# Bank-to-bank copies in 15 groups, an 18th group, one start per bank, and a new order of work

## The chip, the core and the metric

The kernel runs on one core of a Trainium2 chip. The engines of the core are PE (TensorE, the matrix products), DVE (VectorE), ACT (ScalarE), POOL (GpSimd, here the queue that issues the loads) and SP (SyncE, here the queue of the transposes by DMA and of the stores). PE writes its sums into PSUM, which has 8 banks; DVE and ACT read them there and can write there too. The metric is the device time of one execution in microseconds.

## The reference

Attention of 4 batches with 8 heads over 768 tokens, in which a token sees the first 8 tokens and the last 96, with a bias by distance, and then a feed-forward layer with a squared relu:

```python
scores = scale * np.matmul(q, k.transpose(0, 1, 3, 2))
keep = is_global | is_local            # first 8 tokens, or rel in 0..95
scores = scores + bias                 # -slope(head) * distance
a = softmax(np.where(keep, scores, -1e9))
x = np.matmul(a, v)                    # to (3072 tokens, 512)
h = np.maximum(x @ w_in, 0.0)          # 512 -> 2048
out = h * h @ w_out                    # 2048 -> 512
```

Inputs and output are float32; the products take float16.

## The kernel before

**Tiling.** The 3072 tokens are 8 halves (0 to 7) of 384 tokens, two to a batch, each of three tiles of 128. For each half the kernel loads k, q and v (three loads of 128 tokens each, `sk`, `sq` and `v`, issued by POOL), turns k and q so that the head dimension lies on the partitions (by PE in the opening, by two DMA transposes on SP from half 3 on), multiplies them (`score_unit`, L715), takes the exponential on ACT and the mask on DVE, multiplies with v (`attend`, L776), divides on DVE and turns the result into `xt` with four DMA transposes on SP, one for each pair of heads. Then comes layer 1 (`xt` times `w_in`, relu, square, giving `h`) and layer 2 (`h` times `w_out`, giving `y`, which SP stores). Both weight matrices are loaded in four quarters each, by POOL, among the first loads.

**Groups.** Layer 1 of a half has 16 tiles of hidden units. A plain tile (`layer1`, L822) is 4 matmuls over 384 token columns and takes a bank, a relu and half of a square. A group (`layer1_group`, L925) does four such tiles together as a two by two block product by Winograd's form of Strassen's method: 7 products of 4 matmuls over 192 columns each in place of 8, with sums of weights (`in_mix`) and of tokens (`x_mix`) that DVE forms beforehand. The products are named p1, p2, p5, p6, p3, p7, p4. Each adds into a bank; what several results share is kept in between. p1 is needed twice: it goes on in bank `a` for the next products, and it belongs to the first result, which p2 completes. In a plain group p1's sums are kept in SBUF (`keep1`, a copy on ACT or DVE, L353 or L355), p2 runs in a fresh bank `c`, and an instruction of DVE adds the two with the relu (`add_relu`, L983). In a seeded group (`SEEDS` 1) p1's kept sums are copied back into bank `f`, after its last use, and p2 adds to them there; a plain relu (L989 on ACT, L991 on DVE) follows. Squares are L1005 on ACT and L1007 on DVE. Half 2 has two groups, which are seeded, and halves 3 to 7 have three each, which are not: 17 in all. `LAYER1` gives the sequence of a half's layer 1: "s" is a plain tile, and the letters are the products of the three possible groups.

Layer 2 does most of its work in the same way, two token tiles at a time (`layer2_pair`, L1145, 8 matmuls over 256 columns to a product), with `PAIR_SEEDS` for its seeds.

**Order.** All work is first listed as jobs, and then emitted in the sequence of the string `ORDER`. Its words are an engine (`p` PE, `a` ACT, `d` DVE, `s` SP, `l` a load on POOL) and the job's number in the list of PE jobs, of loads, or of all the rest. Digits behind a dot are the banks that the job takes (two for the jobs of scores, one for other jobs that begin a bank). `@` and a number behind a load say that the load waits until the DMA of that job on SP is done: a gate, of which there are eight. Each engine executes its words in this sequence and waits where a word's inputs, its bank or its buffer isn't there yet. `Plan` keeps track of which job uses which bank.

In the opening (the first 20 us) the list has PE's warm-up (p0), the first transposes (p1, p3), products that write distances into banks (p5, p2, p10, p12, p13; they need eight small tables of slopes, d15 to d22 on DVE or ACT), scores, attends (p14 is the first) and transposes to `xt` (p53 is one of the last). Of DVE's words there, d13 forms the distances, d14 is a cast of them, d5, d7, d9 and d11 are casts of the first `sk` and `sq` tiles, and d3 fills a column of `v` and must be done before a load of `v` (l4 and l0 are the first two) may start. The first quarter of `w_in` is l11, the second l13, then l16 and l17. Loads l49 to l54 are the k and q of half 5, l55 to l57 its v, l58 to l63 the k and q of half 6.

Of the kernel before, what the change touches and what calls it, by code (L numbers as in the profile page):

```python
# [9 lines left out]
FP32 = mybir.dt.float32  # L10
# [4 lines left out]
P = 128  # L15
# [24 lines left out]
SEEDS = [0, 0, 1, 0, 0, 0, 0, 0]  # L40
PAIR_SEEDS = [1, 0, 0, 0, 0, 1, 1, 0, 1, 0, 0]
# [4 lines left out]
LAYER1 = {2: "sasbcsdABCsesDEsFGfsgs", 3: "as123456b7cdsAeBCfgDsEFsG",  # L46
# [7 lines left out]
ORDER = """d1 s8 g2 a4 p0.0 a6 s10 d12 a0 d13 l1 d3 l4 l2 l3 d146 a26 d15 d20 a22 l0 a30 d9 d21 a18 d5 a17  # L54
a16 d14 a19 p1.12 a27 p5.34 a28 d11 l5 a29 p10.56 l9 d7 a23 l7 p3 l8 p4.7 l6 d32 a31 a24 d37 p6
d33 a34 p2.07 a39 d35 d36 p7 a40 p11 l10 a25 a41 p8.2 d43 p9.1 p13.34 a46 p12.20 d44 p17 l11 a42
d45 p14.1 d59 a47 l12 p15 d48 a52 p16.5 p24.7 p19.6 d51 p20.3 a49 l13 d55 a53 p18.1 p21.2 d64 l14
a50 p28.5 p23.64 d56 d38 a69 p27.7 d54 l16 p31.0 a57 p26.5 p34.32 a60 d72 l17 p29.6 d68 a61 p35.1
d70 p22.0 d58 l15 l18 a81 p25.4 p30.3 a85 p36.7 d65 a82 p39.16 a86 d71 a66 p32.02 a92 p33.47 d67
d63 p40.35 a77 d84 d91 p38.1 a78 d83 d62 d80 p37.4 l19 a73 d79 a74 p44.7 l22 p41.0 a93 d107 d87  # L60
d76 p47.2 a97 p52.6 p45.7 a89 l21 l23 d111 l20 l27 d96 a119 p48.3 a98 d75 l28 a101 p46.4 l29 p43.1
d110 p53.6 p42.2 d105 l30 d95 p50.5 p55.0 a103 l25 p49.4 d116 d94 a120 a112 p59.1 l24 a102 d88
d106 a90 p51.5 a108 d189 p60.2 a114 d100 a104 d99 p56.6 a113 d191 a122 p57.3 p65.7 d125 p54.4 d138
a117 p63.0 p62.5 a128 d121 a109 p58.1 d139 d129 d130 p61.3 a118 p67.7 d115 a132 d133 d272 a131
p70.4 a135 p71.2 a126 a142 p72.3 p69.0 d162 d127 p82.5 d190 a156 d192 a165 p66.1 a159 l31 a157
a160 p64.7 d205 d158 l26 d163 a123 d161 p84.0 d134 a140 d206 l36 d143 a166 p83.4 d207 a136 l35
d164 p81.6 a167 d187 a141 p85 l33 d124 a137 d186 p79.21 l34 l32 a184 d147 p88.37 p80.45 a178 p77.6
a195 p74.2 a181 d201 d202 a196 d204 p68.3 d203 a179 d151 a182 p73.4 d208 d180 a144 p90.7 l39 d183
a145 p86 a174 a168 d152 a169 p75.1 d154 p78.53 d153 p89.64 p87 a175 d148 a198 p100.2 a176 d155
a193 d150 p98.5 l38 p91.6 a185 d197 a199 d228 p76.3 a209 d177 a210 l37 p96.0 s229 a171 d200 p92  # L70
d172 d225 a173 s194 p93.5 s216 p94 d170 a188 d149 a211 p95.4 d236 s217 p105.1 d219 p97 d214 d237
d212 s220 p102.3 a240 p104 a245 p103.0 s226 d213 d238 a244 d227 d223 d221 p101 d218 p106 l45 a222
p99 l41@226 d246 a241 s215 d243 p109.54 p110.70 s224 l44 a234 p108.36 a251 d239 p111 d258 p118.5
a252 a248 a249 d250 p107 d273 p116.43 p113 a255 l42 p112 a268 l43@217 a256 d253 d230 d254 p119.6
l40 d257 d231 a269 p114.74 l47 p115.03 p124 a261 d274 l46 s235 p120 a283 d259 a264 d270 s275
p122.6 a262 p129.7 d280 p121.2 s242 s325 a265 d232 p127.0 d267 p126 d276 a287 p133.4 d285 d295
a286 d263 s324 p117.3 a290 d233 p130 p123.1 a278 p140 d266 a271 p132 d281 a307 p135 a291 p134.4
p128.2 d298 p136 d294 a279 p131.3 d300 s282 a299 s247 p137.6 a308 l48@324 a297 p138 a303 d323 d301
p139 p125.1 a302 p142 d288 d304 a292 p143.4 d305 a310 d311 p141.6 d326 l49 s296 a284 a312 p144.7
a309 d293 s289 l52 a306 p145.23 d313 p146.05 p147.14 l50 a327 d318 p148.6 a333 d433 d319 a322 l54  # L80
p149.2 a330 d336 a328 d314 l53 p151.16 d320 a331 p150.03 p152 a337 d329 l51 a338 d332 p157.5 a339
p153 d321 a341 d316 a344 a350 a334 p172.0 l65 d315 a342 d345 p159.3 d340 p158.1 p161 d335 a355
p164.2 a352 p155.4 d370 p154.6 p163 a347 d351 s371 p168.0 d395 p162 p169.1 d317 d358 a364 p156
a348 s398 p174.0 d356 a366 d343 a365 p171.4 d359 s399 l56 p177 p160.3 s277 d369 a378 p165 l55 a360
p167 d357 s346 d353 a363 p173.2 p166.4 a372 p178.5 a362 s260 d373 p175 d349 a361 p180 d375 p182.3
s374 p179 d382 a379 p176 p170 d380 p183 d385 p181.0 a381 s354 p184 a376 a383 s386 p185.5 d367 d400
# [3 lines left out]
p197.2 a434 d396 l74 a423 p219.7 d392 a432 d412 a427 d394 p210 d480 d429 p218.6 a445 d477 a462  # L90
d424 p208 a461 p204.4 d431 a448 p205.3 d421 p215.1 a444 p203.7 d443 p214 d442 a458 s491 l66 p199.6
p217.4 d457 p209 a451 p220 d435 a463 p202.7 d449 s492 d428 a441 p212.6 p224 a446 d454 p201 p207.3
a460 d481 d425 s436 a439 p200.7 d482 a471 p221 a447 p213 p216.6 d437 p222.5 d456 s438 d459 d478
p211 a464 d489 l64 p223 d467 a469 p227.2 a484 a493 p229.7 d452 p225 d465 p230 s455 l70@455 d483
a466 p228.6 d453 p232.05 d450 s468 a472 s490 p231.34 d473 d495 s440 d479 a500 l68 s430 l72 l67
l69@455 d470 p226 p234 a501 d496 a497 d502 p235 d494 a474 p233.05 d508 p236.31 a498 d506 p237.64
a503 p239 d475 d485 p249.7 l71 s573 s574 s507 l73 a512 d499 a509 p241.0 p240.6 a520 p245.3 d487
a513 p243.2 d569 d486 a523 a504 d527 p248.4 a510 d488 p270.5 d515 a522 p252 d525 a530 p268.3 d514
a536 a531 p247 d511 p257 a529 p253 d516 p246.1 p254.4 d537 a528 d505 p256 a539 p258.2 a563 d560
p251 a540 p238.7 d517 d543 a545 p242.4 a538 d534 p250.3 a519 d535 p260.5 a524 d532 p267 p255.1  # L100
d544 p261 p266.3 d518 a548 s521 a564 d547 d541 p269 a558 p244 d556 a559 p262 p271 d526 p264 s542
a561 p259.0 d576 a575 p272 d577 d553 s557 p263.1 d546 p276 a562 s533 d551 p265 a589 p273.36 d549
a554 d578 p274.01 s552 a550 p275.45 d555 p277 a582 d593 s570 p278.2 a583 d594 a586 p279.0 d597
s572 a579 d595 p283 a580 s590 d584 s571 l75 a587 d591 p281.14 d598 d585 p280.36 p282.75 a602 d588
s592 p286 a599 d581 p304.1 a600 d609 d596 a603 p301.3 a606 d658 p287.6 a638 p288 d565 a633 d566
a614 d568 p292.4 d615 p307.7 d612 a621 p294 d567 p289.1 a613 d604 a607 p296 d616 p290.3 a624
p314.5 d608 p291 d618 p300 s617 d605 a619 p303.1 d632 s620 p305.3 d652 a637 p308.0 a640 p316 d626
s653 a639 p312.1 p285.5 a611 p309 d648 p297.4 a643 p284.1 a644 d656 p293 a627 s649 d642 p311 d601
p298.5 a610 d628 a657 p310 p299 d647 d629 p313 a631 p317.6 d650 s630 d622 s623 a651 d645 d661 a662
p318.7 d667 p319.5 p306 p295.3 p302 d659 p320 p331.2 a668 d634 p328.0 d625 a646 d641 p315 d635  # L110
a669 p333.7 a691 d660 p329.3 p332.4 d688 d693 p321 a689 d654 a636 d663 d692 a655 d664 p334.7 d665
p336.1 d677 p337 a696 d678 p322 a697 p342 d672 p340 d694 p344.3 d666 p338.4 d673 d705 p339 a698
# [34 lines left out]
class Plan:  # L147
# [153 lines left out]
def kernel(  # L301
# [11 lines left out]
    nc = tc.nc  # L313
# [5 lines left out]
    NPAIR = H // 2  # L319
# [1366 lines left out]
```

## Time and profile before

| | |
|---|---|
| median of 3 runs | 202.17 us (201.56 to 202.5) |
| profiled execution, whole | 201.98 us |
| its span in the profile | 200.2 us |
| granted PE clock | 1.00 |
| score jobs after the opening | 33, in 13 blocks |
| groups, pairs of token tiles | 17, 11 |

The span is the time from the first to the last instruction of the program in the profile. "Busy" is the share in which an engine had an instruction under way; matmuls overlap in a pipeline, so their lengths add up to more than the time in which they run. The chain follows the last instruction back to what released it, step by step.

### The profile page before, as it was taken

To read this page: it belongs to the slowest core of one execution; us is meant where nothing else is said; L and a number is where in the kernel's file an instruction comes from. 1 tells how busy PE (TensorE), PEld (TensorE's weight loads), DVE (VectorE), ACT (ScalarE), POOL (GpSimd) and SP (SyncE) were. 2 spreads that over 40 slices of the span, in tenths; PEclk is the share of its full clock that TensorE was granted. 3 is DMA by queue.
4 is the path that set the end of the run, shared out by engine and by line. 5 is a ranking of instruction groups with operands and counts; after the bars stand their busy time and mean duration, and the time that the engine had idled before them with its cause. 6 is when DMAs were issued, how large, how long until landed. Compare 5 with 4: busy or idle time off the path is not lost.

```text
span 200.2 us, 5881 instructions
## 1 busy us (share of the span) xinstructions
PE 191.8 (96%) x2349; PEld 160.8 (80%) x2349; DVE 177.7 (89%) x448; ACT 146.3 (73%) x310; POOL 66.6 (33%) x82
## 2 busy tenths in 40 slices
PE   7797999999999999999999998999999999999993
PEld 3575899856888687789877897889879899889992
DVE  6889778999995989999999997999999899899780
ACT  6899857998836679988888758987986866365311
POOL 5998537537102910970108700670000000000000
PEclk9999999999999999999999999999999999999999
DMA  5999999999998999999999995699734420020214
GB/s 161 177 149 181 198 181 171 207 194 155 149 224 89 143 123 243 134 149 105 272 119 93 152 140 114 146 150 155 199 75 142 105 75 2 0 108 0 108 52 157
DMA packets 106987, 27.52 MB, mean 137 GB/s; under 512 B 97104, under 2 KB 104016, under 8 KB 106960
## 3 DMA queue, kind: packets, MB, share of 16 engines
q0 software_dynamic: 74944, 13.11, 87.4%
q1 hardware_dynamic: 30816, 13.45, 32.1%
q10 hardware_dynamic: 1200, 0.59, 1.1%
q8 instruction: 18, 0.29, 0.7%
q14 instruction: 9, 0.07, 0.2%
HBM read 27.26 MB, written 6.29 MB: 168 GB/s over the span
## 4 chain that ended last, share of the span: by engine, by line
PE 76%; DMA 13%; POOL 6%; DVE 3%; issue 1%; SPq 0%; ACT 0%; POOLq 0%; DVEq 0%
PE yps L1145 29%; PE hps L822 17%; PE hps L925 17%; DMA w_in_sb<-in_moe_w_in_dram 5%; PE sp L715 4%; PE av L776 4%; PE yps L1059 4%; DMA q<-sq 3%; DMA xt<-tm 3%; DMA v<-in_v_dram 3%; POOL w_mix L491 2%; POOL v L491 2%; DVE hr L983 1%; PE trp L650 1%; POOL sk L491 1%
## 5 line engine op out<-in xcount | busy, mean ns | idle before, releaser
L822 PE MATMUL hps<-xt,w_in_sb 128*128 128x384 f16 (+2 forms) x336 | 45.3, 281 | 0.8 <-DMA w_in_sb<-in_moe_w_in_dram 0.8
L728 ACT ACTIVATE ex<-sp 128x512 f16<-128x512 f32 x66 | 35.3, 619 | 4.4 <-PE sp L715 3.6
L1145 PEld LDWEIGHTS <-h 128*128 128x128 f16 x376 | 34.1, 98 | 4.7
L822 PEld LDWEIGHTS <-w_in_sb 128*128 128x128 f16 x336 | 28.0, 98 | 8.7 <-DMA w_in_sb<-in_moe_w_in_dram 1.2
L1145 PEld LDWEIGHTS <-mixed 128*128 128x128 f16 x272 | 25.1, 98 | 3.1 <-DVE mixed L1110 0.2
L847 ACT ACTIVATE hr<-hps 128x384 f16<-128x384 f32 (+1 forms) x43 | 21.7, 548 | 7.6 <-PE hps L822 7.6
L983 DVE CUSTOM_DVE_ANT_0 hr<-hps,kept 128x384 f16<-128x384 f32 x49 | 25.8, 549 | 1.1 <-PE hps L925 0.7
L491 POOL DMA_DIRECT2D sq<-in_q_dram x19 | 17.0, 900 | 27.2 <-DMA xt<-tm 13.2
L353 ACT COPY kept<-hps 128x384 f32<-128x384 f32 x43 | 20.3, 491 | 7.9 <-PE hps L925 5.8
L353 ACT COPY y<-yps 128x256 f32<-128x256 f32 (+2 forms) x36 | 12.7, 381 | 18.0 <-PE yps L1145 16.5
L491 POOL DMA_DIRECT2D v<-in_v_dram x24 | 21.6, 918 | 12.1 <-DMA k<-sk 9.6
L491 POOL DMA_DIRECT2D sk<-in_k_dram x19 | 17.1, 902 | 25.2 <-DMA xt<-tm 9.4
L925 PEld LDWEIGHTS <-in_mix 128*128 128x128 f16 x272 | 23.0, 98 | 2.4 <-DVE x_mix L903 0.5
L925 PE MATMUL hps<-x_mix,in_mix 128*128 128x192 f16 x204 | 23.7, 247 | 0.2 <-DVE x_mix L903 0.2
L1145 PE MATMUL yps<-w_mix,h 128*128 128x256 f16 (+1 forms) x192 | 22.7, 264 | 0.0
L1145 PE MATMUL yps<-w_out_sb,h 128*128 128x256 f16 (+1 forms) x184 | 22.5, 268 | 0.0
L1145 PE MATMUL yps<-w_mix,mixed 128*128 128x256 f16 (+1 forms) x184 | 22.3, 268 | 0.0
L752 DVE TENSOR_TENSOR phat<-ex,mask 128x1024 f16<-128x1024 f16 (+1 forms) x36 | 21.0, 594 | 0.1
L1005 ACT ACTIVATE h<-hr 128x768 f16<-128x768 f16 x22 | 18.5, 848 | 1.2 <-DVE hr L983 0.7
L925 PEld LDWEIGHTS <-w_in_sb 128*128 128x128 f16 x204 | 17.4, 98 | 1.5
L861 ACT ACTIVATE h<-hr 128x768 f16<-128x768 f16 (+1 forms) x23 | 17.0, 768 | 1.7 <-DVE hr L849 0.9
L925 PE MATMUL hps<-xt,w_in_sb 128*128 128x192 f16 x136 | 15.8, 246 | 0.0
(110 smaller groups left out, 347.9 us busy)
## 6 DMA issues: line engine op xcount, KB each, us to landing
out_dram<-y SPq DMA_DIRECT2D x23, 256.0 KB, 2.6
v<-in_v_dram POOLq DMA_DIRECT2D x24, 128.0 KB, 6.4
sk<-in_k_dram POOLq DMA_DIRECT2D x19, 128.0 KB, 6.0
sq<-in_q_dram POOLq DMA_DIRECT2D x19, 128.0 KB, 5.0
w_in_sb<-in_moe_w_in_dram POOLq DMA_DIRECT2D x4, 512.0 KB, 10.2
w_out_sb<-in_moe_w_out_dram POOLq DMA_DIRECT2D x4, 512.0 KB, 10.5
y<-in_k_dram ACTq DMA_DIRECT2D x2, 256.0 KB, 4.8
y<-in_q_dram SPq DMA_DIRECT2D x2, 256.0 KB, 4.2
```

Source lines behind the costliest of these rows:

```text
L353: nc.scalar.copy(out=out, in_=in_)
L491: dma = nc.gpsimd.dma_start(out=dst, in_=src[x.b, :, r0 + t * P:r0 + (t + 1) * P, :] .rearrange("h p d -> p h d"))
L715: nc.tensor.matmul(sp[h][:, i, :], lhsT=lhsT, rhs=x.q[rows, r % HT, a, :], start=True, stop=True)
L728: nc.scalar.activation(out=st["ex"][:, h], in_=sp[h], func=AF.Exp, scale=scale)
L752: eng(e).tensor_tensor(out=x.phat[a][:, :, t0:t0 + n], op=ALU.mult, in0=st["ex"][:, :, i0:i0 + 2 * n].rearrange("p e (t b) c -> p e t (b c ...
L822: nc.tensor.matmul(st["ps"][:, i * n:(i + 1) * n], lhsT=w_in_sb[:, kk, m * P:(m + 1) * P], rhs=x.xt[:, kk, c0:c1], start=kk == 0, stop=kk ...
L847: nc.scalar.activation(out=o, in_=i, func=AF.Relu)
L861: nc.scalar.activation(out=h2, in_=hr, func=AF.Square)
L925: nc.tensor.matmul(st[name][:, i * HC:(i + 1) * HC], lhsT=left(i, kk), rhs=right(kk), start=fresh and i == kk == 0, stop=kk == KK - 1, ski ...
L983: nc.vector._custom_dve(TENSOR_ADD_SAT, out=hidden(which)[:, :, cols], in0=sums(name), in1=st[kept], s0=LARGEST, s1=0.0)
L1005: nc.scalar.activation(out=h2, in_=hr, func=AF.Square)
L1145: nc.tensor.matmul(st[bank_name][:, 0:n], lhsT=a(m), rhs=b(m)[:, cols], start=fresh and m == 0, stop=m == HK - 1, skip_group_check=not fresh)
```

## The change

The constants: half 2 gets all three groups (seeded as before), and `SEEDS` 2 makes the groups of halves 3 to 7 "copied" ones. In a copied group `across` copies p1's sums from bank `a` into bank `c`, p2 adds to them there with no start flag, and a relu (ACT or DVE) takes the place of `add_relu`. The copy takes its bank when it runs (a word such as `a354.2`), through the new `Plan.copied`. `layer2_pair` gets the same way, but no pair uses it: no entry of `PAIR_SEEDS` is 2.

A matmul with the start flag makes the bank forget what it held, and a product that adds to copied sums must find columns that an earlier product has written since. So scores, attends and layer-1 tiles now set the flag only on the first matmul of a bank, and the order gives the copies banks whose last job wrote all the columns used.

`ORDER` is new throughout. The list of PE jobs has 3 more than before, the list of the rest 4 more, so that in the later halves a job's number is 3 or 4 higher than before (p153 is p150 of before, s358 is s354); loads keep their numbers. There are 16 gates. Words of ACT go from 310 to 306, of DVE from 389 to 397. The diff, cut to its core:

```diff
-SEEDS = [0, 0, 1, 0, 0, 0, 0, 0]
-PAIR_SEEDS = [1, 0, 0, 0, 0, 1, 1, 0, 1, 0, 0]
+SEEDS = [0,0,1,2,2,2,2,2]
+PAIR_SEEDS = [1,0,0,0,0,1,1,0,1,0,0]
...
-LAYER1 = {2: "sasbcsdABCsesDEsFGfsgs", 3: "as123456b7cdsAeBCfgDsEFsG",
+LAYER1 = {2: "1a2b3csd4ABC5es6DEs7FGfsg", 3: "as123456b7cdsAeBCfgDsEFsG",
...
-ORDER = """d1 s8 g2 a4 p0.0 a6 s10 d12 a0 d13 l1 d3 l4 l2 l3 d146 a26 d15 d20 a22 l0 a30 d9 d21 a18 d5 a17
-a16 d14 a19 p1.12 a27 p5.34 a28 d11 l5 a29 p10.56 l9 d7 a23 l7 p3 l8 p4.7 l6 d32 a31 a24 d37 p6
...
-l40 d257 d231 a269 p114.74 l47 p115.03 p124 a261 d274 l46 s235 p120 a283 d259 a264 d270 s275
...
-a387 p186.23 d384 a389 p188.46 d388 l60@371 p187.01 a368 d377 a413 l59@354 p189.7 a406 d401 d405
-l57 a414 d402 p190.4 a409 d404 l62 d403 a407 p191 a410 l63 p193.26 a417 d416 a418 p194.03 d415
-p192.17 l61@386 p195 d476 d411 a419 s390 d391 a426 d408 l58 p196 p206.1 d393 a422 p198.0 d397 a420
...
-p373 a764 a765 s759 p372 d762 s763 p363 a750 s751"""
+ORDER = """d1 a4 a6 a0 s8 s10 d146 g2 l3 l1 d12 d13 a30 d16 a28 a24 d17 l2 p0.0 a19 d14 d5 d15 d22 a18 a25
+a26 a29 d3 d21 d20 d9 p5.34 p1.12 d7 a11 p3 d32 l4 d34 l0 l5 a31 l8 l10 l9 l6 p2.56 a33 p6 p4.7
+a27 a39 d36 d37 d35 p8.0 p7 p13.12 p9.3 d43 a23 a40 p14.7 p10.04 p11 a41 d48 a44 d59 d38 d45 p28.3
...
+d340 d321 a335 a356 p155 d333 a354.2 d336 d324 d320 d326 d339 p153.04 p165 a341 p161 p171.5 p164
+a342 p175.0 a359 p156 a355 d325 p166 d374 p154.20 a368 a348 a343 s375 a345 p159 a346 p176.4 p172.5
+d362 d349 d399 a370.0 p168 p177.2 p158.3 a364 p180 a376 d344 d347 d360 a352 p157.6 d365 p163.7
+d377 p182 p169.3 p174 s350 s402 a382 a351.2 d357 a366 a373 p170 s403 p167 p183 l57@282 d353 p173
+p185.0 d369 p184.7 d384 d386 a361 d385 p186 d437 s358 a367 p178 d389 d379 d371 a363 d372 s260
+p181.4 p187 p179 a391 d404 l62@375 a387 a383 p188.3 a388 p191.05 d392 a380 d381 d405 p195.27 a393
+a417 s378 p189.46 d395 a409 a410 a423 a411 a424 d406 p192.1 s390 d408 p193.0 l61 l60 d407 d420
+p194 l63@358 a418 p197.62 p196.47 p190.15 d419 d412 l58@402 a421 d422 a426 a413 p198 d397 d396
+d433 d484 a427 d401 p208.4 p199 d435 a448 d428 p200.7 a430 a436.6 p222.1 p205.0 d425 a414 p211
...
+d762 p363 p375 p371.7 p376 a768 d742 d751 d747 s763 d744 d766 p366 d754 d760 s743 s767 s755 p374
+a769 d764 s765"""
...
+    def copied(self, job, costs, emit, needs=()):
+
+        op = self.after(job, costs, emit, needs)
+        op.takes, op.users = 1, [[op]]
+        return op
...
                     nc.tensor.matmul(sp[h][:, i, :], lhsT=lhsT, rhs=x.q[rows, r % HT, a, :],
-                                     start=True, stop=True)
+                                     start=i == 0, stop=i == len(unit) - 1,
+                                     skip_group_check=True)
...
     def layer1_group(x, g):
         st, ops, m0, far = {}, {}, 2 * g, NFT // 2
-        seeded = SEEDS[x.hb]
+        seeded, copied = SEEDS[x.hb] == 1, SEEDS[x.hb] == 2
...
         def p1():
-            keep(run("a", True, weight(0, 0), plain(0, 0)), "a", "keep1")
+            job = run("a", True, weight(0, 0), plain(0, 0))
+            if not copied:
+                keep(job, "a", "keep1")
+                return
+
+            def across(e):
+                st["c"] = bank([P, 512], FP32, "hps")
+                copy(e, sums("c"), sums("a"))
+            ops["keep1"] = plan.copied(job, {"ACT": 0.41, "DVE": 0.48}, across)
+            st["users", "c"] = ops["keep1"].users
 
         def p2():
-            if seeded:
+            if copied:
+                give(run("c", False, weight(1, 0), plain(1, 0), [ops["keep1"]]), "c", 0, 0)
+            elif seeded:
                 give(run("f", False, weight(1, 0), plain(1, 0), [ops["seed"]]), "f", 0, 0)
             else:
                 give(run("c", True, weight(1, 0), plain(1, 0)), "c", 0, 0, "keep1")
```

More of the change, by code (lines that the diff above doesn't have):

```diff
@@ L59 @@
[L59 to L70, printed above, removed]
@@ L77 @@
[L77 to L82, printed above, removed]
@@ L95 @@
[L95 to L100, printed above, removed]
@@ L775, in emit @@
                             else x.phat0[:, h, a, :])
-                    nc.tensor.matmul(av[:, h, j, :], lhsT=lhsT, rhs=rhs, start=not before,
-                                     stop=before or r == 0)
+                    nc.tensor.matmul(av[:, h, j, :], lhsT=lhsT, rhs=rhs,
+                                     start=h == 0 and (j, before) == blocks[0],
+                                     stop=h == 1 and (j, before) == blocks[-1],
+                                     skip_group_check=True)
         job = plan.pe(0.0305 * 2 * len(blocks), emit, x.weighs[a] + x.v_in
@@ L1126, in layer2_pair @@
         y_bufs = Buffer("y", 4), Buffer("y", 4)
-        seeded = PAIR_SEEDS[len(seeds)] and not final
+        seeded = PAIR_SEEDS[len(seeds)] == 1 and not final
+        copied = PAIR_SEEDS[len(seeds)] == 2 and not final
         seeds.append(seeded)
@@ L1238, in p1, with across @@
             x.h2_buf.used_by(job)
-            keep(job, "a", "keep1")
+            if not copied:
+                keep(job, "a", "keep1")
+                return
+            def across(e):
+                st["c"] = bank([P, 512], FP32, "yps")
+                copy(e, st["c"][:, 0:HN], st["a"][:, 0:HN])
+            ops["keep1"] = plan.copied(job, {"ACT": 0.31, "DVE": 0.36}, across)
+            st["users", "c"] = ops["keep1"].users
         def p2():
-            if seeded:
+            if copied:
+                job = run("c", False, plain(x, i, 1), weight(1, 0), [ops["keep1"]])
+            elif seeded:
                 job = run("f", False, plain(x, i, 1), weight(1, 0), [ops["seed"]])
@@ L1246, in p2 @@
             x.h2_buf.used_by(job)
-            give(job, "f" if seeded else "c", 0, 0, None if seeded else "keep1")
+            give(job, "f" if seeded else "c", 0, 0, None if seeded or copied else "keep1")
         def p5():
@@ L1411, in emit @@
                     nc.tensor.matmul(pair[h][:, a, :], lhsT=lhsT, rhs=halves[r // HT].q[rows, r % HT, a, :],
-                                     start=not added, stop=not added or a == NPAIR - 1,
-                                     skip_group_check=added)
+                                     start=not added and a == 0, stop=a == NPAIR - 1,
+                                     skip_group_check=True)
         needs = list(tile_ops[r])
```

92 lines of the change are left out of this document (56 added, 36 removed).

## The prediction

> **What bounds the kernel now.** First the page's busy times and the chain that ended last, then the windows of the whole span.
>
> ```profile
> PE 191.8 (96%) x2349; PEld 160.8 (80%) x2349; DVE 177.7 (89%) x448; ACT 146.3 (73%) x310; POOL 66.6 (33%) x82
> PE 76%; DMA 13%; POOL 6%; DVE 3%; issue 1%; SPq 0%; ACT 0%; POOLq 0%; DVEq 0%
> 35.00:106.00 71.00, 71.00 (x847) 56.39 (x845) 66.02 (x160) 57.22 (x124) 26.10 (x31) 1.00 1.62 165
> 106.00:123.00 17.00, 16.12 (x203) 13.95 (x202) 16.72 (x44) 12.57 (x27) 7.63 (x9) 1.00 1.55 129
> 123.00:186.00 63.00, 63.00 (x729) 56.04 (x729) 58.55 (x138) 45.99 (x90) 6.99 (x8) 1.00 0.56 94
> ```
>
> PE holds 76% of the chain. In the windows (length, then PE, PEld, DVE, ACT and POOL busy, granted clock) it is busy without a gap from 35 to 106 us and from 123 to 186 us, at clock 1.00; only 106 to 123 us lacks 0.88 us. A busy PE need not be a fast one, so I look at how far its pieces lie apart, in the chain in order of time (start, length, line, matmuls):
>
> ```profile
> 65.79 0.33 PE sp L715 x8
> 66.12 0.98 PE yps L1145 x8
> ...
> 70.18 0.66 PE hps L925 x8
> 70.84 0.65 PE hps L822 x4
> ...
> 81.31 0.78 PE sp L715 x24
> ...
> 83.94 0.55 PE sp L715 x16
> ...
> 85.80 0.87 PE yps L1145 x8
> ```
>
> Pieces abut, and one kind costs the same wherever it stands: a group's product of 4 matmuls over 192 columns 0.33 us, a plain layer-1 tile of 4 over 384 columns 0.65, a pair's product of 8 over 256 columns 0.87. So past 35 us PE's own work sets the time, and a wait counts only where it opens a hole in PE.
>
> The Trainium skill (Perfetto Trace Analysis, Identifying the Most-Contended Engine) says that busy matmuls are a poor measure and that the weight load's share is a good one; by its 80% PE would have headroom, and products saved or added below would be worth nothing: the sum would be -0.96 us in place of -1.05. The abutting pieces speak against that here.
>
> The holes between 106 and 123 us stand in PE's timeline, and what leads to them in the waits and the chain:
>
> ```profile
> 107.24 0.81 PE L822 MATMUL hps<-xt,w_in_sb 128*128 128x384 f16 x4
> 108.22 0.51 PE L925 MATMUL hps<-x_mix,in_mix 128*128 128x192 f16 x4 [0.16 <-DVE x_mix L903]
> ...
> 111.28 0.19 PE L776 MATMUL av<-vb,phat 128*128 128x65 f16 x1
> 111.62 0.19 PE L776 MATMUL av<-v,phat 128*128 128x65 f16 x1
> ...
> 120.73 1.04 PE L1145 MATMUL yps<-w_out_sb,h 128*128 128x256 f16 x8
> 122.34 0.57 PE L715 MATMUL sp<-q,k 64*128 64x128 f16 x14 [0.57 <-DMA q<-sq]
> ```
> ```profile
> POOL sk L491 <- DMA xt<-tm: 9.4, 2, 6.6
> ```
> ```profile
> 100.06 5.36 DMA xt<-tm
> 106.57 5.01 DMA v<-in_v_dram
> 116.73 5.47 DMA q<-sq
> ```
>
> From starts: the four 384-column matmuls need 0.65, so the next was due at 107.89 and came 0.33 late; the av matmuls stand 0.03 apart, here 0.34: 0.31 lost; the eight from 120.73 need 0.87, so the scores were due at 121.60 and came 0.74 late, 0.10 of it usual (next part): 0.64. The last two have one cause. A sk load stood 6.6 us on POOL behind an xt transpose (word l59@354) until 105.42; behind it were a v load of half 5 (l57, landed 111.6) and four more of the six loads that half 6's turns need (l62 l63 l61 l58), so those turns came late too (q landed 122.2).
>
> **The change part by part.** *The 18th group* (half 2) takes 7 products of 0.33 for 4 plain tiles of 0.65: 2.31 - 2.60 = -0.30 with the unrounded pieces.
>
> *Score blocks.* In the rows above blocks of 8, 16 and 24 score matmuls take 0.33, 0.55 and 0.78: 0.225 for each 8 and 0.10 to enter; a pair's product right behind one takes 0.98, not 0.87: 0.11 to leave. Score jobs are the PE words with two bank digits. After the opening the old order has them in 13 blocks, the new one, with p153.04 and p154.20 apart, in 14: +0.21.
>
> *DMA gates.* In the new order l57 stands ahead of the gated sk and sq loads, and half 6's six stand as l62@375 l61 l60 l63@358 l58@402 l59. Behind the xt transpose of pair 2 (word 358, 354 before) are three loads, not six, and SP issues it right behind half 5's turns, with no other transpose and no stores between. The late v and q should both be early by microseconds: -0.31 - 0.64 = -0.95. I don't count the 0.33 at the x_mix (xt pair 3 comes one store earlier); I set it against waits that 16 gates in place of 8 may open elsewhere. Bounds: all three holes go and none comes, -1.28; none goes and one as large as the largest comes, +0.64.
>
> *Copies and reliefs.*
>
> ```profile
> L353 ACT COPY kept<-hps 128x384 f32<-128x384 f32 x43 | 20.3, 491 | 7.9 <-PE hps L925 5.8 <-DVE hr L983 1.6
> L353 ACT COPY hps<-kept 128x384 f32<-128x384 f32 x2 | 1.0, 482 | 0.5 <-DVE hr L983 0.5
> L355 DVE COPY kept<-hps 128x384 f32<-128x384 f32 x8 | 4.4, 552 | 0.9 <-PE hps L925 0.9
> L983 DVE CUSTOM_DVE_ANT_0 hr<-hps,kept 128x384 f16<-128x384 f32 x49 | 25.8, 549 | 1.1 <-PE hps L925 0.7 <-ACT h L1005 0.2
> L989 ACT ACTIVATE hr<-hps 128x384 f16<-128x384 f32 x13 | 6.4, 489 | 2.1 <-PE hps L925 2.1
> L1005 ACT ACTIVATE h<-hr 128x768 f16<-128x768 f16 x22 | 18.5, 848 | 1.2 <-DVE hr L983 0.7 <-DVE hr L991 0.4
> L1007 DVE TENSOR_TENSOR h<-hr 128x768 f16<-128x768 f16 x12 | 6.5, 552 | 0.2
> ```
>
> No row copies from bank to bank. Bank to memory takes ACT 491 ns, memory to bank 482; a copy with both ends in banks lies between 482 (nothing more) and 973 (both in full). I take 490, the nearest row, and 550 on DVE; 13 of the 15 stand on ACT, 2 on DVE, as their keep1 copies did. Each hold becomes a copy, and each add with relu (DVE, 549) a relu: 10 on ACT (489), 5 on DVE. That frees 5.5 us of DVE, and the order spends it: 8 group squares and 3 plain ones move from ACT (848) to DVE (552), 6 second keeps too; some ten smaller ones go the other way. My count gives DVE's sum +0.1 us and ACT's -4.8. Neither paces PE past 35 us (windows), so 0 here.
>
> On the path a copy counts only where its second product waits. Between first and second product the new order has at least two group products and one pair's, 0.33 + 0.33 + 0.87 = 1.53 us of PE work, in the three closest groups, and up to 5.8. A copy with its hand-overs (0.49 + about 0.2, an estimate) fits, at its upper bound too. Without that cover each group would cost some 0.7. The bank is held longer, but from the last product in a bank to the next PE job that takes it the least PE work between is 0.88 us (0.79 before). So 0; bounds 0 and +0.5. The fewer start flags change no instruction count: 0.
>
> *The opening.*
>
> ```profile
> 3.74 0.88 POOL L491 DMA_DIRECT2D v<-in_v_dram x1 [1.32 <-DVE slope_id L430]
> 12.54 0.81 POOL L555 DMA_DIRECT2D w_in_sb<-in_moe_w_in_dram x1
> ...
> 4.87 0.88 DVE L355 CAST sk<-y 128x512 f16<-128x512 f32 x1
> 5.67 0.34 DVE L424 CAST early<-dmask 128x384 f16<-128x384 f32 x1
> ...
> 12.17 0.30 PE L1461 MATMUL av<-v,ph 128*128 128x65 f16 x4
> ...
> 20.02 1.94 PE L822 MATMUL hps<-xt,w_in_sb 128*128 128x256 f16 x24 [0.64 <-DMA w_in_sb<-in_moe_w_in_dram]
> 23.62 1.92 PE L822 MATMUL hps<-xt,w_in_sb 128*128 128x256 f16 x16 [0.19 <-DMA w_in_sb<-in_moe_w_in_dram]
> ```
> ```profile
> v<-in_v_dram POOLq DMA_DIRECT2D x1, 128.0 KB, 5.0
> sk<-in_k_dram POOLq DMA_DIRECT2D x1, 128.0 KB, 3.5
> ```
>
> PE twice waits for a quarter of w_in. Loads leave POOL 0.87 us apart. The load of v (l4) needs the memset d3; before it was second, at 3.74, and the first quarter tenth behind it, at 12.54. Now l4 is fourth and the quarter eighth behind it, but d3 stands behind the casts d14 (0.34, early) and d5 (sk): if sk's cast runs as before, 4.87 to 5.75, then two slopes and the memset follow, some 0.4, so l4 leaves near 6.2 and the quarter near 6.2 + 7.0 = 13.2, 0.6 late. Loads in the opening landed 5.0 us after their issue, a lone one (105.7 us) after 3.5; so some 1.5 us of queue ahead should swallow that. By the second quarter PE has also done one more transpose pair (p53, 0.11). I take -0.06; bounds -0.11 and +0.8.
>
> *The tail.*
>
> ```profile
> 196.82 0.37 ACT L353 COPY y<-yps 128x256 f32<-128x256 f32 x1 [1.05 <-PE yps L1145]
> ...
> L1207 DVE TENSOR_TENSOR y<-yps,y 128x256 f32<-128x256 f32 x28 | 11.2, 417 | 2.5 <-ACT ex L728 1.4 <-PE yps L1145 1.0
> ```
>
> The last evacuation was that copy (0.37); now it is an add on DVE (d764, 0.42): +0.05, the same store behind it.
>
> **Sum.** -0.30 + 0.21 - 0.95 - 0.06 + 0.05 = -1.05 us against the profiled execution's 201.98 (span 200.2): 200.93. The median shown is 202.17, 0.19 above it; from there 201.1, which I give. A measurement of this kernel tells about 0.5% (1.01 us) from no change.
>
> **The rivals.**
>
> *The waits move instead of going.* Other gated loads or the twice reordered SP queue open holes of the same size. For it: 16 gates, and the h7 loads wait on transposes of half 5 and 6. Against: after 123 us POOL issues 8 loads only (windows). Time: 202.17 - 0.10 (sum without the 0.95) = 202.1, or about 201.6 with half of it.
>
> *The opening slips* (slower). The mechanism is d3 behind d5: v leaves at 6.2 or later, lands at 11, and PE's attend p14, now in front of 27 other opening jobs, waits for it; at the same time p5, now PE's first job after the warm-up, waits for the last slopes behind d3. From p14 to the first layer-1 product the old run took 12.17 to 20.02 (rows above); the new one has four more jobs there (some 1.9 us with entries), so it needs p14 by about 10.7. Each later start goes one to one to the end, as everything from 20 us on is without slack but for 0.2 to 0.6 at the quarters. With p14 1.6 late and the waits still there: 202.17 - 0.04 + 1.6 = 203.7; with the waits gone 202.8. It decides from p14 at about 12. Against it: v's landing at 5.0 behind 6.2 is 11.2, within the slack.
>
> *Copies on the path.* If copies took 973 ns and ACT stood late, the three tightest groups could lose 0.3 each: 201.1 + 0.9 = 202.0. ACT's lower load speaks against it.
>
> *More goes than I count*: the 0.33 too and 0.3 in the opening: 200.5.
>
> **How the numbers follow.** Forecast 201.1 (200.6 to 201.6) 0.52; more goes 0.10; waits move 0.22; opening slips 0.12, most of it slower than 203.2 or near; copies on the path 0.04. The forecast's case lies across the 0.5% bound (201.16): 0.37 of its 0.52 below. So faster 0.37 + 0.10 = 0.47; same 0.15 + 0.22 + 0.03 = 0.40 (a slight slip and a part of the copies stay there); slower 0.13. The range takes in all holes gone (202.17 - 1.05 - 0.33 - 0.3 and the spread of the runs) and a slip of about 0.9 with the waits kept: 200.2 to 202.9.
>
> **What would show it.** Right: PE windows full between 106 and 123 us, no wait on q<-sq, POOL's longest wait on xt gone, 14 score blocks, 126 group products x 4 matmuls at 0.33, bank-to-bank copies near 490 ns, first quarter of w_in used near 20.0. Wrong: the first layer-1 matmul later than 20.6; new gaps in PE behind L715 or L776; copies near 970 ns with PE waiting on ACT before L925.

## The result and the profile after

| | before | after |
|---|---|---|
| median | 202.07 us (200.54 to 204.42, 20 runs) | 203.42 us (202.15 to 206.25, 20 runs) |
| profiled execution, whole | 201.98 us | 202.16 us |
| its span | 200.2 us | 200.4 us |

The ratio of after to before is 1.0063, with a 95% interval from 1.0034 to 1.0092: slower, where 201.1 us had been forecast. The ratios here and below leave out the slow runs, those more than 1.5% above the fastest of their kernel. The profiled execution of after is nearly the fastest of its 20 runs, 1.26 us below their median. What the median adds has to come from further runs.

First the lines of after's page that answer to those shown of before: the busy times and the chain by engine.

```profile
PE 193.8 (97%) x2359; PEld 162.1 (81%) x2359; DVE 178.0 (89%) x457; ACT 141.1 (70%) x305; POOL 66.5 (33%) x82
PE 77%; DMA 8%; DVE 7%; POOL 4%; issue 2%; DVEq 0%
```

DVE's sum rose by 0.3 us and ACT's fell by 5.2, about as counted (+0.1, -4.8). Now after's windows (start and end, length, then PE, PEld, DVE, ACT and POOL busy with their counts, granted clock, DMA share, GB/s).

```profile
0.00:20.00 20.00, 18.23 (x243) 11.96 (x243) 15.77 (x56) 16.35 (x35) 17.00 (x25) 1.00 1.69 164
20.00:35.00 15.00, 14.56 (x199) 12.90 (x195) 12.22 (x38) 9.94 (x21) 8.41 (x11) 1.00 1.80 183
35.00:106.00 71.00, 70.20 (x860) 56.74 (x859) 66.25 (x161) 58.17 (x126) 30.52 (x35) 1.00 1.63 165
106.00:123.00 17.00, 17.00 (x215) 15.06 (x213) 16.74 (x47) 11.97 (x28) 5.27 (x7) 1.00 1.84 162
123.00:186.00 63.00, 62.92 (x730) 55.69 (x728) 59.69 (x141) 42.08 (x90) 5.29 (x7) 1.00 0.54 86
```

The stretch from 106 to 123 us is full, as forecast: the waits for x_mix, v and q are gone. But the stretch from 35 to 106 us, full in before, now lacks 0.80 us. After's waits of PE (what waited, on what: us in total, times, longest) say for what:

```profile
PE yps L1169 <- DVE y L1231: 0.5, 1, 0.5
PE hps L832 <- DMA w_in_sb<-in_moe_w_in_dram: 0.4, 1, 0.4
PE sp L722 <- DMA q<-sq: 0.3, 1, 0.3
```

The first and the third are new holes: by the starts PE was due at 64.7 and 62.9 us. After's timelines of PE, DVE and POOL (start, length, engine, line, operation, in brackets the idle time before it and what ended it) show where the opening slipped and why DVE was late:

```profile
20.56 1.05 PE L832 MATMUL hps<-xt,w_in_sb 128*128 128x256 f16 x8 [0.44 <-DMA w_in_sb<-in_moe_w_in_dram]
65.45 0.81 PE L1169 MATMUL yps<-w_mix,h 128*128 128x256 f16 x6 [0.53 <-DVE y L1231]
```
```profile
4.84 0.43 DVE L362 CAST sk<-y 128x512 f16<-128x512 f32 x1 [0.49 <-DMA y<-in_k_dram]
5.18 0.56 DVE L437 TENSOR_SCALAR slope_id<-ident 128x128 f16<-128x128 f16 x4
5.59 0.10 DVE L512 MEMSET v<- 128x48 f16 x1
...
64.37 0.36 DVE L915 TENSOR_TENSOR x_mix<-xt 128x384 f16<-128x384 f16 x1 [1.96 <-DMA xt<-tm]
```
```profile
5.98 1.75 POOL L498 DMA_DIRECT2D v<-in_v_dram  x2 [1.82 <-DVE slope_id L437]
...
13.00 0.77 POOL L562 DMA_DIRECT2D w_in_sb<-in_moe_w_in_dram  x1
```

The memset d3 stands behind the sk cast, which waits for its input, and POOL stands for it 1.82 us. Every load behind it on POOL is late with it: the first quarter of `w_in` left at 13.00 in place of 12.54, and the first layer-1 product began at 20.56 in place of 20.02. From there to the start of PE's last matmul before took 176.49 us and this execution of after 176.03: 0.46 less, so in this execution the rest of the change did gain, and the opening took it away. The median of the runs is over a microsecond above this one, and that the single trace can't explain.

### The profile page after: what moved, and what is told of

The parts are those of the page before. It is cut to its first block, busy times and chain, and to the rows that moved or that the text cites. A ratio compares the mean times of both kernels' runs of the same rounds, so it can differ in the third digit from the quotient of the medians.

```text
span 200.4 us, 5912 instructions
## 1 busy us (share of the span) xinstructions
PE 193.8 (97%) x2359; PEld 162.1 (81%) x2359; DVE 178.0 (89%) x457; ACT 141.1 (70%) x305; POOL 66.5 (33%) x82
## 4 chain that ended last, share of the span: by engine, by line
PE 77%; DMA 8%; DVE 7%; POOL 4%; issue 2%; DVEq 0%
PE yps L1169 27%; PE hps L937 20%; PE hps L832 18%; PE av L784 4%; DMA w_in_sb<-in_moe_w_in_dram 4%; PE sp L722 4%; PE yps L1082 3%; DMA xt<-tm 2%; POOL w_mix L498 2%; DMA y<-in_k_dram 2%; POOL v L498 1%; DVE y L1231 1%; DVE mixed L1133 1%; PE av L1495 1%; DVE tm L796 1%
## 5 line engine op out<-in xcount | busy, mean ns | idle before, releaser
L832 PE MATMUL hps<-xt,w_in_sb 128*128 128x384 f16 (+2 forms) x320 | 42.8, 278 | 0.4 <-DMA w_in_sb<-in_moe_w_in_dram 0.4
L832 PEld LDWEIGHTS <-w_in_sb 128*128 128x128 f16 x320 | 26.1, 98 | 6.9 <-DMA w_in_sb<-in_moe_w_in_dram 0.6
L360 ACT COPY y<-yps 128x256 f32<-128x256 f32 (+2 forms) x39 | 14.3, 378 | 18.7 <-PE yps L1169 17.9
L937 PEld LDWEIGHTS <-in_mix 128*128 128x128 f16 x288 | 24.5, 98 | 1.9
L937 PE MATMUL hps<-x_mix,in_mix 128*128 128x192 f16 x216 | 25.1, 246 | 0.0
L995 DVE CUSTOM_DVE_ANT_0 hr<-hps,kept 128x384 f16<-128x384 f32 x36 | 18.9, 548 | 1.4 <-PE hps L937 0.9
L937 PEld LDWEIGHTS <-w_in_sb 128*128 128x128 f16 x216 | 18.5, 98 | 1.3
L937 PE MATMUL hps<-xt,w_in_sb 128*128 128x192 f16 x144 | 17.3, 246 | 0.0
L1001 ACT ACTIVATE hr<-hps 128x384 f16<-128x384 f32 x27 | 13.0, 494 | 4.9 <-PE hps L937 4.8
L360 ACT COPY kept<-hps 128x384 f32<-128x384 f32 x28 | 13.2, 484 | 3.7 <-PE hps L937 3.5
L1231 DVE TENSOR_TENSOR y<-yps,y 128x256 f32<-128x256 f32 (+1 forms) x30 | 12.0, 407 | 2.6 <-PE yps L1169 2.2
```

What stands on the lines that cost most here:

```text
L360: nc.scalar.copy(out=out, in_=in_)
L832: nc.tensor.matmul(st["ps"][:, i * n:(i + 1) * n], lhsT=w_in_sb[:, kk, m * P:(m + 1) * P], rhs=x.xt[:, kk, c0:c1], start=kk == 0 and i == ...
L937: nc.tensor.matmul(st[name][:, i * HC:(i + 1) * HC], lhsT=left(i, kk), rhs=right(kk), start=fresh and i == kk == 0, stop=kk == KK - 1, ski ...
L995: nc.vector._custom_dve(TENSOR_ADD_SAT, out=hidden(which)[:, :, cols], in0=sums(name), in1=st[kept], s0=LARGEST, s1=0.0)
L1001: nc.scalar.activation(out=o, in_=i, func=AF.Relu)
L1231: eng(e).tensor_tensor(out=y, in0=ps, in1=y, op=ALU.add)
```

## Experiments

Theory A: the new order puts DMA landings on PE's path, by late loads in the opening and by words of DVE that wait for a landing ahead of words that PE needs. Theory B, its rival: the copies from bank to bank cost time on PE. Every ratio is to runs of the kernel before on the same chip, with its 95% interval.

**The change once more, unchanged.**

> The changed kernel once more, for a second profile and its spread. Theory A (the new order sets waits in the path of DMA landings: first loads in the opening 0.5 us late, VectorE held by the x_mix of half 2 at 62 to 65 us): 1.004 to 1.009 of the kernel before, the first layer-1 matmul again near 20.5 us instead of 20.0, and a VectorE wait on an xt transpose of 1 to 3 us before 66 us, longer where the run is slower. Theory B (the copies from bank to bank cost time on PE): the same ratio, but holes in PE spread over halves 3 to 7, before L937 matmuls.

Measured: 204.35 us (202.84 to 206.07), ratio 1.0069 (1.0029 to 1.0109). Its profiled execution took 205.01 us, above the median, and so shows what the first trace lacked. Against the expectation its first layer-1 product came at 20.05 us, not near 20.5; it lost its time later. Its waits of PE:

```profile
PE yps L1169 <- DVE mixed L1133: 1.7, 1, 1.7
...
PE sp L722 <- DMA q<-sq: 1.0, 1, 1.0
PE av L1495 <- DMA v<-in_v_dram: 0.7, 1, 0.7
```

and its timelines of DVE and PE around the largest:

```profile
102.76 0.69 DVE L1133 TENSOR_TENSOR mixed<-h 128x1024 f16<-128x1024 f16 x1
105.51 0.36 DVE L915 TENSOR_TENSOR x_mix<-xt 128x384 f16<-128x384 f16 x1 [2.06 <-DMA xt<-tm]
105.78 0.68 DVE L1133 TENSOR_TENSOR mixed<-mixed,h 128x1024 f16<-128x1024 f16 x1
```
```profile
106.53 1.05 PE L1169 MATMUL yps<-w_mix,mixed 128*128 128x256 f16 x8 [1.74 <-DVE mixed L1133]
```

The same thing as at 64 us, at another place: DVE stands 2 us at an x_mix whose `xt` hasn't landed, and a word that PE needs is queued behind it. These are waits on DMA landings, each of 0.3 to 1.9 us, at places where before had none.

**One such wait taken away.** Half 2's x_mix goes behind the y additions on DVE:

```diff
-d230 ... d246 ... d227
+d246 ... d227 d230
```

> The changed kernel with one word moved: the first x_mix of half 2 (d230) stands on VectorE behind the two y adds that it stood ahead of. Theory A: the hole of 0.69 us in PE at 64.6 us goes, so 0.5 to 0.8 us less than the changed kernel in the same call (a ratio to the kernel before lower by 0.003 to 0.004), more if slow runs wait there longer. Theory B: no difference over 0.2 us.

Measured: 203.34 us (202.18 to 205.25), ratio 1.0050 (1.0014 to 1.0085). The hole behind 64.7 us is gone from its trace, and others stand elsewhere. The ratio is 0.0019 below that of the unchanged kernel, where 0.003 to 0.004 was expected, and the intervals overlap. One wait of this kind is worth too little to tell.

**The memset early.**

```diff
-... d12 d13 a30 ... a26 a29 d3 d21 ...
+... d12 d13 d3 a30 ... a26 a29 d21 ...
```

> The changed kernel with one word moved: the memset d3, which a load of v needs, stands on VectorE right behind the distances, as in the kernel before. Theory A: POOL's fourth load leaves at 4.1 to 4.2 us in place of 5.98, the first quarter of w_in lands 0.5 us or more earlier, and the first layer-1 matmul stands near 20.0 in place of 20.56: 0.3 to 0.6 us less than the changed kernel. If PE's own opening is the bound instead, the quarter lands early and the first layer-1 matmul stays within 0.2 us.

Measured: 201.51 us (200.2 to 203.27), ratio 0.9948 (0.9915 to 0.9982); once more on another chip (its expectation stands below) 202.06 us, ratio 0.9957 (0.9928 to 0.9986). One memset of 0.10 us, moved, is worth 201.51 - 204.35 = -2.84 us by the medians of one chip, 0.0121 or 2.4 us by the ratios, and 0.0095 or 1.9 us on the other chip (against dmid, below). That is far more than the 0.3 to 0.6 us expected, and the kernel is now faster than before. Its timeline of POOL:

```profile
4.15 1.77 POOL L498 DMA_DIRECT2D v<-in_v_dram  x2
...
11.30 0.80 POOL L562 DMA_DIRECT2D w_in_sb<-in_moe_w_in_dram  x1
```

No wait is shown before v's load, and `w_in` leaves 1.7 us earlier than in after. With the x_mix moved too:

> The changed kernel with v's column cleared early on VectorE (as in d3) and with half 2's x_mix word behind the y additions (as in xmix). Theory A, in its narrowed form (the 2.8 us between d3 and the unchanged new order are all the price of the 1.8 us by which GpSimd's loads leave later; the hole at 64.6 us exists only with late loads): within 0.3 us of d3, ratio near 0.995, no hole of over 0.3 us in PE between 60 and 70 us in either. Rival (the x_mix word is a cost of its own): 0.5 to 1 us below d3, ratio near 0.991.

Measured: 202.35 us (200.36 to 205.07), ratio 0.9971 (0.9936 to 1.0006); 0.0023 above d3, so the rival's gain of 0.5 us or more isn't there, and the x_mix word is no cost of its own that these runs could tell. Against the expectation this trace has a hole of 0.7 us at 62 us (`PE sp L722`, on `q<-sq`); the last section returns to it.

**Are the copies a cost?** Nine of the 15 copied groups get kept sums in SBUF and the addition on DVE back (the other six stay as they are), first in the change as it is, then with the memset early:

```diff
+HELD = [(3, 3), (3, 1), (4, 2), (4, 3), (5, 1), (5, 2), (5, 3), (6, 3), (7, 3)]
...
-        seeded, copied = SEEDS[x.hb] == 1, SEEDS[x.hb] == 2
+        seeded, copied = SEEDS[x.hb] == 1, SEEDS[x.hb] == 2 and (x.hb, g) not in HELD
```

In the order `a354.2 ... p161 ... a355` becomes `a354 ... p161.2 ... d355`, and so for each of the nine.

> The changed kernel with 9 of its 15 copied groups (halves 3 to 7) put back to the kept sums and the add with relu on VectorE, in the same order of work and the same banks. Theory A: within 0.3 us of the changed kernel, VectorE's sum up by some 3 us (relus that ran on ScalarE become adds on VectorE). Theory B: faster than the changed kernel by 0.5 us or more, PE's holes in halves 3 to 7 gone.

Measured: 206.00 us (205.23 to 206.93), ratio 1.0163 (1.0113 to 1.0213).

> The changed kernel with v's column cleared early, and 9 of the 15 copied groups back on kept sums in SBUF with the addition on VectorE. If the bank-to-bank copies are worth something by themselves (VectorE rid of 9 additions): 1 to 2 us above d3, ratio 1.000 to 1.005, with holes before h's products that wait on VectorE's additions. If hold lost its 1.65 us against the unchanged new order only since late loads had pushed VectorE's work together: within 0.4 us of d3, ratio near 0.995. Theory B (copies cost PE time): below d3.

Measured: 204.33 us (203.3 to 205.15), ratio 1.0088 (1.0058 to 1.0119). In both the copies' absence costs: 1.65 us in hold, where theory A had expected no more than 0.3, and 1.3 to 1.4% in d3hold (1.0088 against 0.9948 and 0.9957; 1.2% against d3xmix on its own chip). The largest wait of PE in d3hold:

```profile
PE hps L938 <- DVE hr L996: 1.5, 2, 1.0
```

PE stands at products of a group for DVE's additions. So theory B falls: in this order the copies spare time. It is no measure of what they bring over the old order, which was laid out for kept sums.

**How much delay costs how much.** The memset goes to three more places, and once the opening's loads stand as before has them:

```diff
 dmid:   ... d5 d3 d15 d22 ...
 dlate:  ... d5 d15 d22 ... d21 d20 d9 d3 ...
 open_b: ... d13 l1 d3 l4 l2 l3 ... (in place of l3 l1 d12 d13 ... l2 ... d3 ... l4)
```

> The changed kernel with v's column cleared right behind the d5 cast, ahead of the slope words d15 and d22: v's load should leave near 5.6 us and w_in's first quarter near 12.6, as late as in the kernel before (12.54). Linear theory (2.8 us at the end for 1.8 us of load delay, all along): 1.9 to 2.1 us above d3, ratio near 1.004. Threshold theory (what was forecast: the queue that the kernel before had swallows a delay up to there, and the cost begins behind it): within 0.5 us of d3, ratio 0.994 to 0.997.

> The changed kernel with v's column cleared later still, behind the cast d9 of the first q: v's load near 6.4 us, w_in's first quarter near 13.4, 0.4 us behind the unchanged new order. Linear theory: 0.5 to 0.7 us above the unchanged new order, ratio near 1.010. Threshold theory with a steep cost behind 12.6 us: 1 us or more above it, ratio 1.012 or more. Rival (the cost has its full size once any turn is missed): as the unchanged new order, ratio near 1.007.

> The kernel of d3 once more, beside the two others on one chip. Theory A: ratio 0.993 to 0.998, as in d3 (0.9948) and, with one VectorE word moved, d3xmix (0.9971). Rival (d3's gain was of its chip): 0.998 or more.

> The changed kernel with GpSimd's first loads and the clearing of v's column in the places that the kernel before gives them (k, the clearing, v, k, q): v's load near 3.7 us, w_in's first quarter near 12.5 us, as in before; all behind the opening is the change. Forecast's theory (with the opening as before, the sum of its other terms stands): 0.9 to 1.1 us below before, ratio near 0.995. Linear theory (a line through d3 at 11.3 us and the unchanged new order at 13.0 to 13.1): ratio near 1.003. Rival (v's load is what matters, not w_in's: it leaves at 3.7 us, ahead of d3's 4.15): as d3, 0.995, with w_in as late as in before.

The timeline of POOL in dmid:

```profile
5.96 1.90 POOL L498 DMA_DIRECT2D v<-in_v_dram  x2 [1.61 <-DVE slope_id L437]
...
13.16 0.76 POOL L562 DMA_DIRECT2D w_in_sb<-in_moe_w_in_dram  x1
```

dmid misses its aim: behind the sk cast the memset is as late as in the change, so this is a third run of the change, and it agrees with the other two. With it the kernels of the new order, by when the first quarter of `w_in` leaves POOL:

| kernel | w_in leaves, us | ratio | interval |
|---|---|---|---|
| d3, d3 again | 11.30, 11.29 | 0.9948, 0.9957 | 0.9915 to 0.9982, 0.9928 to 0.9986 |
| open_b | 12.44 | 1.0012 | 0.9984 to 1.0040 |
| after, again, dmid | 13.00, 13.10, 13.16 | 1.0063, 1.0069, 1.0052 | 1.0016 (lowest) to 1.0109 (highest) |
| dlate | 13.80 | 1.0100 | 1.0065 to 1.0135 |

From the first row to the third the ratio rises by 0.0109 (1.0061 less 0.9952) in 1.79 us, 0.0061 or 1.2 us for each microsecond of delay. That line gives 1.0022 at 12.44 and 1.0105 at 13.80, and both runs lie on it within their intervals. A queue that swallows the delay up to before's 12.54, as forecast, would leave open_b at d3's 0.995, and it isn't there. A shorter flat stretch isn't excluded, nor are dlate's rivals (1.007 and 1.012 lie in its interval). The third theory, that v's load matters and not that of `w_in`, doesn't fit either: in open_b v left at 3.74 us, ahead of d3's 4.15. open_b has a weakness: the new order's first products on PE expect q first, and its first layer-1 product came only at 21.19. It speaks against the forecast's theory (0.995 lies outside its interval), but isn't the pure case.

**The same in the old order.**

```diff
-b_early: ... d13 l1 d3 l4 l2 l3 ...
+b_early: ... d13 l3 l1 l2 d3 l4 ...
-b_late:  ... d13 l1 d3 l4 l2 l3 ... d5 ...
+b_late:  ... d13 l3 l1 l2 ... d5 d3 l4 l0 ...
```

> The kernel before, with nothing of the change but the column of v cleared early on VectorE and the order of the first loads that lets GpSimd's leave early (q and k ahead of v). w_in's first quarter issued near 11.3 us instead of 12.54, the first layer-1 product near 19.3 to 19.8 instead of 20.02. Theory A (each 1 us by which GpSimd's loads move is worth about 1.5 us at the end): 0.5 to 1.8 us below before, ratio 0.991 to 0.997. Rival (before had queue enough: the opening costs only what the first product waits, and before waited little): within 0.4 us of before, ratio 0.998 to 1.002.

> The kernel before, with nothing of the change but the clearing of v's column put behind the d5 cast on VectorE, as the change has it: w_in's first quarter issued near 13.0 us instead of 12.54. Theory A (the memset's place alone makes the cost, in the old order too): 0.5 to 1.5 us above before, ratio 1.0025 to 1.0075. Rival (the cost needs the change's other moves too): within 0.4 us of before, ratio 0.998 to 1.002.

Measured: b_early 203.0 us, ratio 1.0022 (0.9989 to 1.0055); b_late 204.58 us, ratio 1.0076 (1.0037 to 1.0115). Both have the new sequence of the first loads (l3 l1 l2), so they differ by the memset, with the loads l4 and l0 that follow it: `w_in` left at 11.54 and at 12.95. The late memset costs in the old order as well, 0.0054 or 1.1 us between the two. But loads that leave 1.0 us earlier than before's bring nothing there, and the first layer-1 product came at 20.17, not at the 19.3 to 19.8 expected. The waits of PE in b_early show why:

```profile
PE sp L715 <- DMA q<-sq: 1.6, 1, 1.6
PE hps L822 <- DMA xt<-tm: 1.3, 1, 1.3
```

The first is the hole of before behind 121.6 us, the gated turn of half 6, now 1.6 us long: PE came earlier to a landing that had not moved. In this execution the old order's gates hold back what the early opening gains; in d3 nothing holds it back there. At late loads the new order is worth nothing (after 1.0063, again 1.0069, b_late 1.0076); at early ones about 0.0070 (1.0022 less 0.9952), 1.4 us.

## Why the prediction was wrong

**Where the time went.** The holes of each trace, as in the prediction: from each matmul's start to the next, less the length of its kind, summed where over 0.05 us, without the entries and exits of score blocks, from the first layer-1 product on. "Work" is the time from there to PE's last product without the holes and without those entries and exits.

| kernel | first layer-1 product | holes to 75 us | 75 to 112 | behind 112 | score blocks | work |
|---|---|---|---|---|---|---|
| before | 20.02 | 0.54 | 0.85 | 0.83 | 2.70 | 171.57 |
| after | 20.56 | 1.43 | 0 | 0.41 | 2.93 | 171.26 |
| again | 20.05 | 2.96 | 2.29 | 0.08 | 2.81 | 171.25 |
| dmid | 20.63 | 1.92 | 1.47 | 0.32 | 2.91 | 171.27 |
| d3 | 20.11 | 0.14 | 0 | 0.08 | 3.03 | 171.28 |
| d3 again | 19.99 | 0.21 | 1.27 | 0.24 | 2.91 | 171.23 |
| b_early | 20.17 | 0.29 | 0.15 | 3.57 | 2.71 | 171.53 |

The three executions with late loads lose 3.6 us in holes on average (1.84, 5.33, 3.71), before lost 2.2, those with the early memset 1.2 (0.22, 1.72, and 1.6 in d3xmix). Only a part of the delay shows at the first layer-1 product of these three, 0.4 us on average (20.41 against 20.02); the larger part falls due later. It needn't: in xmix and dlate the first layer-1 product came at 21.24 and 22.28 us, and the holes behind it are 2.2 and 1.4 us. So a late load costs at once in one execution and later in another. Windows of dmid, then of d3 again, show the later holes directly:

```profile
20.00:35.00 15.00, 14.06 (x194) 12.27 (x190) 11.70 (x37) 10.12 (x22) 8.17 (x10) 1.00 1.79 183
35.00:80.00 45.00, 44.50 (x530) 34.78 (x528) 41.91 (x102) 34.87 (x78) 16.73 (x20) 1.00 1.64 168
80.00:110.00 30.00, 28.72 (x366) 24.63 (x364) 27.89 (x67) 25.18 (x56) 15.75 (x18) 1.00 1.59 152
```
```profile
20.00:35.00 15.00, 15.00 (x203) 13.38 (x202) 12.70 (x39) 9.76 (x22) 8.76 (x11) 1.00 1.80 183
35.00:80.00 45.00, 45.00 (x539) 35.17 (x538) 42.79 (x105) 36.93 (x80) 17.13 (x21) 1.00 1.61 174
80.00:110.00 30.00, 29.25 (x364) 24.58 (x359) 28.51 (x68) 25.39 (x56) 14.81 (x17) 1.00 1.64 151
```

dmid's PE stands 0.94, 0.50 and 1.28 us in the three stretches, d3 again's 0, 0 and 0.75.

Not every one of these holes is owed to the late loads. The one at 62 us stands where half 3's `q<-sq` took over 5 us to land, and d3xmix has it with early loads. The 1.74 us of again at 106 us stand behind an `xt` transpose that took 4.1 us to land, and 2.3 in after. The hole at 86 us of d3 again is on an `xt` transpose too, with early loads. The last section shows what goes with such landings. So the medians show what the memset's place costs; how much of it each hole carries is only argued, from single executions.

**Point by point.**

- *The opening* is the first step that failed. The forecast saw the mechanism (d3 behind the sk cast) and sized its first effect well: `w_in` forecast at 13.2, measured 13.00 to 13.16. It then let 1.5 us of queue swallow the 0.6, for -0.06. The runs show no such swallowing: by the 1.2 us for each microsecond, the 0.46 to 0.62 of delay against before are 0.6 to 0.7 us. The forecast priced one load, the first quarter, and one waiter, the first layer-1 product. All loads behind the memset were late, those of v for the attends at 21 us among them (holes of 0.9 us in again and 1.0 in dmid). Half 3's turn of q then left 0.2 us later in after than in d3, 1.3 in again and 1.0 in dmid. But these 0.6 to 0.7 us are the smaller part of the 2.3 us between forecast and result.
- *The rival "the opening slips"* had the mechanism and its sign, with 0.12. Its place was wrong: the first attend, which it has at about 12 us, began at 11.29 in after, 10.55 in again and 11.08 in dmid, ahead of before's 12.17, and what cost time were waits from 20 to 106 us. That its 203.7, with the old waits still there, lies near 203.42 is luck.
- *The DMA gates*, -0.95, is the second step that failed, and the larger. The three holes went in after, as forecast. But waits of the same kind opened elsewhere, where DVE stands at an x_mix ahead of words that PE needs, and where PE reaches half 3's scores before its q. The forecast set 0.33 against them. Over after, again and dmid the holes rose from before's 2.2 to 3.6 us, +1.4 in place of -0.95. With early loads they fell to 1.2 on average, about as forecast, but not in every execution: up to 112 us from 1.39 to 0.14 in d3, and to 1.48 in d3 again. With loads as late as before's, where the forecast has -0.99 (the sum without the opening), the line gives 1.0028 or +0.6 us.
- *The rival "the waits move instead of going"*, with 0.22, had what became of this term, but not its size: 202.1 is 1.3 us short, and it looked for the new waits at gated loads and in the SP queue, not on DVE.
- *The 18th group*, -0.30: work fell from 171.57 to between 171.23 and 171.28, by 0.29 to 0.34. *The score blocks*, +0.21: they rose from 2.70 to between 2.81 and 3.03, by 0.11 to 0.33. Both as priced.
- *The tail*, +0.05: after ended 200.4 - 196.59 = 3.81 us behind the start of PE's last matmul, before 200.2 - 196.51 = 3.69: +0.12.
- *The copies*, 0 on the path. After's groups on ACT and DVE (count, busy us and mean ns):

```profile
L360 ACT COPY hps<-hps 128x384 f32<-128x384 f32 x13 | 6.1, 471 | 3.0 <-PE hps L937 1.0 <-DVE hr L995 0.8 <-ACT ex L736 0.5
L362 DVE COPY hps<-hps 128x384 f32<-128x384 f32 x2 | 1.1, 562 | 0.0
L995 DVE CUSTOM_DVE_ANT_0 hr<-hps,kept 128x384 f16<-128x384 f32 x36 | 18.9, 548 | 1.4 <-PE hps L937 0.9 <-ACT y L360 0.3
```

471 ns, forecast 490, and none of PE's waits in after (above) names a copy. That DVE's relief is worth 0 can't be said: with nine additions back on DVE the new order loses 1.65 us and more.

- *The weight load's share.* By the rule of the Trainium skill that the prediction set against the trace (Perfetto Trace Analysis, Identifying the Most-Contended Engine) PE, with its weight loads at 81%, would have headroom. If that meant slack in which a late load could hide, the runs decide against it: each microsecond of delay came out as 1.2 at the end.

**What stays open.** The early memset puts the loads 1.2 us ahead of before's, not level with them. No run shows the new order with before's loads and PE's first products in the order that fits them; the line through the others gives 1.003 at 12.54 us, open_b 1.0012. So a gain of the rest of the change is shown for early loads only. Why 0.5 us of delay against before turned a forecast gain of 1.05 us into a loss of 1.3 is settled in part: the memset's place decides the sign, but the waits that make up the sum were read from one execution each.

The fastest version run is the change with the early memset, 0.9948 and 0.9957 of before.

## What to carry to other kernels

Where one queue issues all loads, an instruction that one early load waits for delays all that stand behind it: price the delay for every later load and its waiter, not for the first one. On an engine without slack, look for where it will stand next, since a wait removed late in the kernel leaves room for an earlier one, and what an earlier opening gains can stop at a gate further on. One profile shows where PE stood in that execution; what an edit is worth takes the times of many. Small words such as a memset belong ahead of words that wait for data, not behind them.

## What the runs showed of the hardware

The same transpose by DMA can take two quite different times. Half 3's `q<-sq` in d3 and in d3xmix (line, engine, operation, count, issue time in ns, start; then us from issue to landing):

```profile
L677 SPq DMA_TRANSPOSE q<-sq x1: 1455/1455/1455, 57.6 to 57.6; - x1
...
DMA to landing us min/median/max: 3.7/3.7/3.7
```
```profile
L677 SPq DMA_TRANSPOSE q<-sq x1: 1456/1456/1456, 57.5 to 57.5; - x1
...
DMA to landing us min/median/max: 5.4/5.4/5.4
```

It was issued at the same time in both, and landed 1.7 us later in the second, which made the hole there. What goes with it stands in the DMA answers of the traces. d3xmix's, from the issue to the landing, lists a transfer of the queue "instruction", one packet of 16 KB (number, MB, share of 16 engines); d3's, from 57.6 to 61.4 us, lists none:

```profile
q8 instruction: 1, 0.02, 1.4%
```

It is so in all 14 traces. In the ten with such a packet between issue and landing (it takes 0.9 us or more) this transpose took 5.2 to 5.7 us: the five with late loads (after, again, xmix, dmid, dlate), hold, open_b, d3xmix, b_early and b_late. In the four without it took 3.7 to 4.2: before, both executions of d3, and d3hold. An `xt` transpose issued at 98 to 102 us in the new order shows the same: 4.1 and 4.2 us with the packet (again and open_b, which have holes of 1.7 and 1.5 us behind it), 2.3 to 2.4 in the nine others. No run sets when the packet comes, so it is likely the cause, but that isn't shown. It is also a rival, in part, to the late loads: of the new order's four traces with the early memset three escape the packet at half 3's q, of the six with the late one none does.

Executions of one kernel lie 4 us apart (after: 202.15 to 206.25); such landings may be a part of that, and they make one profile a poor witness of where its median goes. And a copy with both ends in PSUM took ACT 471 ns, no more than one from PSUM to SBUF (491 in before, 484 in after).
